# Shared output sub-tiles for the left tokens, a next-to-last q piece in two parts, and q norms by a fused multiply and sum, in an attention and feed-forward kernel

## The chip, the cores and the metric

The kernel runs on one core of one Trainium2 chip. The metric is device time in microseconds (us); lower is better. Beside the device time each execution has a *span*, from the first to the last instruction in the trace. The span is 1.7 to 2.5 us shorter than the device time in the profiled executions, and that difference is not the same for all kernels, which will matter below.

Names: PE is TensorE's matmuls and PEld its weight loads, DVE is VectorE, ACT is ScalarE, POOL is GpSimd, SP is SyncE; ACTq and SPq are DMA issues on the queues of ScalarE and SyncE.

## The reference, cut to what matters

```python
# q, k, v: (4, 5824, 256); w1, w2: (256, 1024); w3: (1024, 1024); w_out: (1024, 256)
qn = q / (norm(q, axis=1, keepdims=True) + 1e-6)     # a norm per channel, over the 5824 tokens
kn = k / (norm(k, axis=1, keepdims=True) + 1e-6)
s  = kn.transpose(0, 2, 1) @ qn / tau                # 256 x 256 per batch
a  = softmax(s, axis=-1)
x  = (v @ a).reshape(4 * 5824, 256)
out = ((x @ w1) * (x @ w2)) @ w3 @ w_out             # float32
```

The kernel folds the softmax result into w1 and w2 (so that `a` and `b` come straight from v), and w3 into w_out. Per batch there are 5824 = 45 x 128 + 64 tokens. They are worked off in 11 large chunks of 512 tokens and one small chunk of 128 + 64; the 64 are the *left* tokens.

## The kernel before

The start of batch 0: squares of q and k and their products G (the scores) on TensorE as the pieces arrive, then the *k row* (`dk` and two small fp32 matmuls, which make a row of the norms of k; it needs k's last piece), then the norm of q; all pieces of q and k are loaded first, then the weights and v. `busy(2)` is a pair of warm-up matmuls whose result nobody uses.

```python
def q_first():
    d = work.tile([P, CT, P], F32, tag="sq", name="dq", bufs=2)
    nc.vector.tensor_mul(d, S["q"], ident.unsqueeze(1).to_broadcast([P, CT, P]))
    ss = work.tile([P, CT], F32, tag="ss0", name="ss0", bufs=1)
    nc.vector.tensor_reduce(out=ss, in_=d, op=ALU.add, axis=mybir.AxisListType.X)
    st["ss"] = ss

def q_norm(src):                                   # r = 1 / (sqrt(src) + 1e-6)
    r = work.tile([P, CT], F32, tag="r", name=f"r_{n}", bufs=2)
    nc.scalar.activation(out=r, in_=src, func=AF.Ln)
    nc.scalar.activation(out=r, in_=r, func=AF.Exp, scale=0.5)
    nc.vector.tensor_scalar_add(r, r, 1e-6)
    nc.vector.reciprocal(r, r)
# ...
load_piece("q", 0, 4)
load_piece("q", 0, 5, (2, 4))
for h in range(2):
    # ... halves of w1 and w2 on the same queue, then half of v's first piece
    load_part("v", 0, 0, h * half, (h + 1) * half)
# ...
squares("k", 5, range(LAST + 1), end=True)
# ... dk, busy(2), the row of k factors
squares("q", 4, whole)
products(4, whole)
```

One step j of a chunk: two products a and b, the copy of a by ScalarE, the product by VectorE, and, two steps later, the output matmuls. PSUM tiles of a and b come from one pool of four buffers (tag "ab").

```python
def emit_ab(b, c, j):
    n = chunk_cols(c)                              # 512, or 192 in the small chunk
    # ... matmuls a and b into tiles[0], tiles[1] (tag "ab", bufs=4)
    nc.scalar.copy(a_sb[:, :n], tiles[0][:, :n])
    ab = work.tile([P, 512], BF16, tag="ab_sb", name=f"abs_{b}_{c}_{j}", bufs=8 * NDEF + 6)
    nc.vector.tensor_mul(ab[:, :n], a_sb[:, :n], tiles[1][:, :n])

def emit_out(b, c, j, ab):
    small = c == NCH - 1
    subs = [0, 64] if small else [0, 128, 256, 384]     # 0:128, and 64:192 for the 64 left ones
    for s, off in enumerate(subs):
        nc.tensor.matmul(tl[s // 2][:, s % 2, :], lhsT=ab[:, off : off + P], rhs=W_sb[:, j, :], ...)
    # at j == FT - 1, small: copy both, store rows on nc.sync (nc.scalar in the last batch),
    # then the 64 left rows on nc.sync
```

In the small chunk the second output matmul covers columns 64 to 191, of which only the last 64 are new.

## Time and profile before

| | before |
|---|---|
| device time, median of 3 | 581.64 us (581.58 to 581.91) |
| profiled execution: time, span | 581.33 us, 579.2 us |
| TensorE busy | 567.8 us, 98% |
| first softmax sum / output copy of batch 0's small chunk / last store issued | 38.12 / 190.31 / 575.95 us |

With TensorE busy nearly all the time, the questions are what the start costs before it can run, and which matmuls can go. In a line of the timeline the columns are start, duration, engine, line, operation, output and inputs, shapes and count; the bracket at the end holds the engine's idle time just before and what ended it. The lines of before stand in the prediction below; this one, from the table of 1 us stretches, shows the clock at 21 us (busy shares of PE, PEld, DVE, ACT, POOL, then granted clock, DMA share, GB/s):

```profile
21.00:22.00 1.00, 1.00 (x8) 0.82 (x7) 0.00 (x0) 0.00 (x0) 0.00 (x0) 0.50 1.04 209
```

The 0.50 is the granted clock: half speed in that microsecond. The 16 products that start at 21.21 take 3.17 us; 16 take 1.91 at full speed.

### The profile page before, as it was taken

To read this page: it belongs to the slowest core of one execution; us is meant where nothing else is said; L and a number is where in the kernel's file an instruction comes from. 1 tells how busy PE (TensorE), PEld (TensorE's weight loads), DVE (VectorE), ACT (ScalarE), POOL (GpSimd) and SP (SyncE) were. 2 spreads that over 40 slices of the span, in tenths; PEclk is the share of its full clock that TensorE was granted. 3 is DMA by queue.
4 is the path that set the end of the run, shared out by engine and by line. 5 is a ranking of instruction groups with operands and counts; after the bars stand their busy time and mean duration, and the time that the engine had idled before them with its cause. 6 is when DMAs were issued, how large, how long until landed. Compare 5 with 4: busy or idle time off the path is not lost.

```text
span 579.2 us, 10219 instructions
## 1 busy us (share of the span) xinstructions
PE 567.8 (98%) x3844; PEld 362.9 (63%) x3844; DVE 376.0 (65%) x569; ACT 341.8 (59%) x628; POOL 64.3 (11%) x141
## 2 busy tenths in 40 slices
PE   8899999999999999999999999999999999999997
PEld 4755667766666566666665666666665756665555
DVE  0047645888877667788766667778876656565564
ACT  0046535777765567677765566777665545454453
POOL 5240021110000202002000112001100000000000
PEclk9899999999999999999999999999999999999999
DMA  8999989773544899655562699754563325301011
GB/s 164 213 206 195 169 152 207 156 171 85 115 104 110 132 222 169 125 110 124 120 135 74 134 200 175 173 112 87 146 127 92 85 76 146 86 38 74 38 69 54
DMA packets 65970, 74.85 MB, mean 129 GB/s; under 512 B 45825, under 2 KB 49793, under 8 KB 65921
## 3 DMA queue, kind: packets, MB, share of 16 engines
q0 software_dynamic: 15232, 39.46, 40.0%
q1 hardware_dynamic: 50544, 34.61, 20.8%
q8 instruction: 30, 0.49, 0.3%
q14 instruction: 20, 0.16, 0.1%
q10 hardware_dynamic: 144, 0.13, 0.1%
HBM read 78.91 MB, written 23.86 MB: 177 GB/s over the span
## 4 chain that ended last, share of the span: by engine, by line
PE 90%; DMA 5%; DVE 2%; ACT 1%; issue 1%; POOL 1%; ACTq 0%; POOLq 0%
PE o L437 27%; PE a L415 26%; PE b L415 26%; PE G L188 5%; DMA q<-in_q_dram 5%; PE fold L341 2%; PE w L547 1%; ACT as L421 1%; DVE abs L423 1%; PE G L233 0%; PE sqq L221 0%; POOL k L109 0%; DVE osb L452 0%; ACT e L304 0%; PE row L269 0%
## 5 line engine op out<-in xcount | busy, mean ns | idle before, releaser
L423 DVE TENSOR_TENSOR abs<-as,b 128x512 bf16<-128x512 bf16 (+1 forms) x384 | 251.9, 658 | 153.5 <-ACT as L421 138.8
L421 ACT CAST as<-a 128x512 bf16<-128x512 f32 (+1 forms) x384 | 215.5, 562 | 173.5 <-PE a L415 85.1
L437 PE MATMUL o<-W_sb,abs 128*128 128x256 bf16 x1472 | 221.5, 273 | 0.5 <-ACT osb L451 0.4
L415 PEld LDWEIGHTS <-Wf 128*128 128x128 bf16 x1536 | 148.8, 98 | 97.2 <-issue 1.7
L415 PE MATMUL a<-vT,Wf 128*128 128x512 bf16 x704 | 209.3, 379 | 0.3
L415 PE MATMUL b<-vT,Wf 128*128 128x512 bf16 x704 | 209.4, 379 | 0.1
L437 PEld LDWEIGHTS <-abs 128*128 128x128 bf16 x1472 | 143.4, 98 | 87.0 <-issue 0.5
L197 DVE TENSOR_TENSOR acc<-acc,sq 128x1024 f32<-128x1024 f32 x66 | 80.4, 1219 | 0.1
L407 POOL COPY gate_t<-abs 1x1 bf16<-1x1 bf16 x39 | 11.2, 287 | 395.9 <-DVE abs L423 379.5
L188 PE MATMUL G<-k,q 128*128 128x256 bf16 x276 | 49.9, 273 | 0.0
L185 ACT ACTIVATE sq<-q 128x512 f32<-128x512 bf16 x66 | 41.8, 633 | 0.0
L185 ACT ACTIVATE sq<-k 128x512 f32<-128x512 bf16 x66 | 41.6, 631 | 0.0
L452 DVE COPY osb<-o 128x512 f32<-128x512 f32 x44 | 30.1, 685 | 0.4 <-PE o L437 0.4
L188 PEld LDWEIGHTS <-q 128*128 128x128 bf16 x276 | 27.0, 98 | 3.1
L451 ACT COPY osb<-o 128x512 f32<-128x512 f32 x44 | 25.7, 585 | 3.8 <-PE o L437 1.7
L271 ACT ACTIVATE kr<-row 128x256 f32<-128x256 f32 x4 | 1.5, 383 | 30.9 <-PE row L269 30.9
L341 PE MATMUL fold<-w,e 128*128 128x512 bf16 x64 | 16.5, 378 | 0.0
L109 POOL DMA_DIRECT2D q<-in_q_dram x27 | 14.5, 538 | 12.8 <-DMA q<-in_q_dram 6.4
L348 ACT ACTIVATE Wf<-fold,rs 128x512 bf16<-128x512 f32 x16 | 10.9, 687 | 7.9 <-PE fold L341 5.7
L109 POOL DMA_DIRECT2D k<-in_k_dram x25 | 13.8, 550 | 3.4 <-DMA k<-in_k_dram 1.9
L109 POOL DMA_DIRECT2D v<-in_v_dram x25 | 13.4, 537 | 6.1 <-issue 4.6
L350 DVE TENSOR_SCALAR Wf<-fold,rs 128x512 bf16<-128x512 f32 x16 | 11.8, 748 | 1.8 <-PE fold L341 1.4
(96 smaller groups left out, 177.4 us busy)
## 6 DMA issues: line engine op xcount, KB each, us to landing
out_dram<-osb SPq DMA_DIRECT2D x44, 512.0 KB, 3.0
k<-in_k_dram POOLq DMA_DIRECT2D x19, 512.0 KB, 9.5
q<-in_q_dram POOLq DMA_DIRECT2D x19, 512.0 KB, 6.2
v<-in_v_dram POOLq DMA_DIRECT2D x19, 512.0 KB, 5.4
w_wout<-in_moe_w_dram POOLq DMA_DIRECT2D x2, 1024.0 KB, 16.3
k<-in_k_dram POOLq DMA_DIRECT2D x4, 320.0 KB, 6.6
v<-in_v_dram POOLq DMA_DIRECT2D x4, 320.0 KB, 5.0
w<-in_moe_w_dram POOLq DMA_DIRECT2D x4, 256.0 KB, 7.2
```

The lines of the kernel that those rows point to most:

```text
L109: nc.gpsimd.dma_start(out=pieces[nm, n, pi][:, lo:hi, :], in_=qk_main[nm, n][0][:, pi * PIECE + lo : pi * PIECE + hi, :])
L185: nc.scalar.activation(out=dst[:, :, part, :], in_=src[:, o : o + 2, :], func=AF.Square)
L188: nc.tensor.matmul(G[:, ct, :], lhsT=qt[:, i, ct * P : (ct + 1) * P], rhs=kt[:, i, :], start=(pr == 0 and part == 0 and ct == 0), stop=(pr ...
L197: nc.vector.tensor_add(accs[n], accs[n], sqs[0])
L341: nc.tensor.matmul(st["fold", i], lhsT=st["e"][:, c2, c1 * P : (c1 + 1) * P], rhs=w12[:, c2, w, h * 512 : (h + 1) * 512], start=(c2 == 0), ...
L350: nc.vector.tensor_scalar_mul(dst, st["fold", i], st["rs"][:, c1 : c1 + 1])
L415: nc.tensor.matmul(t[:, :n], lhsT=Wf[b][:, ct, w, j * P : (j + 1) * P], rhs=rhs_of(b, c, ct), start=(ct == 0), stop=(ct == CT - 1),)
L421: nc.scalar.copy(a_sb[:, :n], tiles[0][:, :n])
L423: nc.vector.tensor_mul(ab[:, :n], a_sb[:, :n], tiles[1][:, :n])
L437: nc.tensor.matmul(tl[s // 2][:, s % 2, :], lhsT=ab[:, off : off + P], rhs=W_sb[:, j, :], start=(j == 0 and s % 2 == 0), stop=(j == FT - 1 ...
L451: nc.scalar.copy(o[:, 0:2, :], tl[0])
L452: nc.vector.tensor_copy(o[:, 2:4, :], tl[1])
```

## The change

The intent has three parts. (1) The left tokens of two batches share one sub-tile of 128 rows, so that the even batches need no second output matmul and the odd ones do a full one. (2) The next-to-last piece of q is loaded in two halves, so that its squares start sooner; three pairs of warm-up matmuls come along. (3) The q norm of batch 0 is one fused multiply-and-sum per half instead of a multiply and a reduce.

```diff
 def q_first():
-            nc.vector.tensor_mul(d, S["q"], ident.unsqueeze(1).to_broadcast([P, CT, P]))
-            nc.vector.tensor_reduce(out=ss, in_=d, op=ALU.add, axis=mybir.AxisListType.X)
+            for ct in range(CT):
+                nc.vector.tensor_tensor_reduce(
+                    out=d[:, ct, :], in0=S["q"][:, ct, :], in1=ident, scale=1.0, scalar=0.0,
+                    op0=ALU.mult, op1=ALU.add, accum_out=ss[:, ct : ct + 1],
+                )
 # emit_ab
-        nc.vector.tensor_mul(ab[:, :n], a_sb[:, :n], tiles[1][:, :n])
+        if n == 4 * P:
+            nc.vector.tensor_mul(ab, a_sb, tiles[1])
+        else:
+            nc.vector.tensor_mul(ab[:, :P], a_sb[:, :P], tiles[1][:, :P])
+            if b % 2 == 0 and j == 0:
+                lefts[b // 2] = work.tile([P, FT, 2, LEFT], BF16, tag="left", name=f"left_{b}", bufs=1)
+            nc.vector.tensor_mul(lefts[b // 2][:, j, b % 2, :], a_sb[:, P:n], tiles[1][:, P:n])
 # emit_out
-        subs = [0, 64] if small else [0, 128, 256, 384]
+        if small:
+            lhs = [ab[:, :P]]
+            if b % 2 == 1:
+                lhs.append(lefts[b // 2][:, j, :, :].rearrange("p b t -> p (b t)"))
 # ... the end of a small chunk, odd batches only
-                nc.sync.dma_start(out=out[b * N + NT * P : (b + 1) * N, :], in_=o[LEFT:, 1, :])
+                    for k in range(2):
+                        m = b - 1 + k
+                        nc.sync.dma_start(
+                            out=out[m * N + NT * P : (m + 1) * N, :], in_=o[k * LEFT : (k + 1) * LEFT, 1, :]
+                        )
 # ... the start of batch 0
     for pi in range(1, 4):
         squares("k", pi, whole)
+        busy(2)
         squares("q", pi, whole)
         products(pi, whole)
-    load_piece("q", 0, 4)
+    load_piece("q", 0, 4, (half,))
 # ...
-    squares("q", 4, whole)
-    products(4, whole)
+    for sl in (lo, hi):
+        squares("q", 4, sl)
+        products(4, sl)
```

More of the change, by code (lines that the diff above doesn't have):

```diff
@@ L46 @@
     assert moe_w_out.shape == (F, D)
-    assert T == B * N
+    assert T == B * N and B % 2 == 0
     CT = C // P
@@ L390 @@
     out_tiles = {}
+    lefts = {}
     pend = []
@@ L429, in emit_out @@
         small = c == NCH - 1
-        subs = [0, 64] if small else [0, 128, 256, 384]
+        if small:
+            lhs = [ab[:, :P]]
+            if b % 2 == 1:
+                lhs.append(lefts[b // 2][:, j, :, :].rearrange("p b t -> p (b t)"))
+        else:
+            lhs = [ab[:, i * P : (i + 1) * P] for i in range(4)]
         if j == 0:
             out_tiles[b, c] = [
-                psum.tile([P, 2, D], F32, tag="out", name=f"o_{b}_{c}_{h}", bufs=3) for h in range(len(subs) // 2)
+                psum.tile([P, 2, D], F32, tag="out", name=f"o_{b}_{c}_{h}", bufs=3) for h in range((len(lhs) + 1) // 2)
             ]
         tl = out_tiles[b, c]
-        for s, off in enumerate(subs):
+        for s, lhsT in enumerate(lhs):
             nc.tensor.matmul(
-                tl[s // 2][:, s % 2, :], lhsT=ab[:, off : off + P], rhs=W_sb[:, j, :],
-                start=(j == 0 and s % 2 == 0), stop=(j == FT - 1 and s % 2 == 1), skip_group_check=True,
+                tl[s // 2][:, s % 2, :], lhsT=lhsT, rhs=W_sb[:, j, :],
+                start=(j == 0 and s % 2 == 0), stop=(j == FT - 1 and (s % 2 == 1 or s == len(lhs) - 1)),
+                skip_group_check=True,
             )
-        clock[0] += len(subs) * (D * MM_COL + MM_FIX)
+        clock[0] += len(lhs) * (D * MM_COL + MM_FIX)
         if j == FT - 1:
@@ L446, in emit_out @@
                 nc.scalar.copy(o[:, 0, :], tl[0][:, 0, :])
-                nc.vector.tensor_copy(o[LEFT:, 1, :], tl[0][LEFT:, 1, :])
                 (nc.scalar if b == B - 1 else nc.sync).dma_start(out=rows[:, NT - 1, :], in_=o[:, 0, :])
-                nc.sync.dma_start(out=out[b * N + NT * P : (b + 1) * N, :], in_=o[LEFT:, 1, :])
+                if b % 2 == 1:
+                    nc.vector.tensor_copy(o[:, 1, :], tl[0][:, 1, :])
+                    for k in range(2):
[3 more added lines that the diff above has]
+                        )
             else:
```

## The prediction

> **What bounds the kernel now.** I read the page first (engines, slices, chain of waits), then the chain in order of time for the first 66 us, then the timeline of the start, of a batch's small last chunk and of the end, then a table of 1 us stretches for the granted clock.
>
> From the page of the kernel before:
> ```profile
> span 579.2 us, 10219 instructions
> PE 567.8 (98%) x3844; PEld 362.9 (63%) x3844; DVE 376.0 (65%) x569; ACT 341.8 (59%) x628; POOL 64.3 (11%) x141
> ...
> PE 90%; DMA 5%; DVE 2%; ACT 1%; issue 1%; POOL 1%; ACTq 0%; POOLq 0%
> ```
> TensorE is the bound: it makes up 90% of the chain that ended last. A matmul taken out after the start is worth its time, unless something takes its place. DMA has 5%: the start, where the loads of the first batch arrive.
>
> The start, from the timeline:
> ```profile
> 29.58 0.42 DVE L244 TENSOR_TENSOR dk<-sqk,ident 128x256 f32<-128x256 f32 x1 [17.80 <-PE sqk L221]
> ...
> 30.06 0.70 PE L269 MATMUL row<-dk,ones_pp 128*128 128x256 f32 x2
> ...
> 31.16 1.07 PE L221 MATMUL sqq<-q 128*128 128x128 bf16 x16 [0.40 <-DMA q<-in_q_dram]
> ...
> 35.77 0.42 DVE L249 TENSOR_TENSOR dq<-sqq,ident 128x256 f32<-128x256 f32 x1 [5.76 <-PE sqq L221]
> ...
> 36.23 0.42 DVE L251 TENSOR_REDUCE ss<-dq 128x2 f32<-128x256 f32 x1
> ...
> 36.82 0.45 PEld L132 LDWEIGHTS <-v 128*128 128x128 bf16 x8 [0.51 <-DMA v<-in_v_dram]
> ...
> 38.12 0.20 PE L320 MATMUL sum<-ones_b,e 128*128 128x1 bf16 x2 [0.67 <-ACT e L304]
> ```
> Piece 4 of q, the next to last, lands just before 31.16; from there TensorE works without a gap to the last square at 35.7. Then the q norm runs through VectorE and ScalarE until the softmax sums at 38.12. All later work hangs on these two.
>
> The small chunk of batch 0, from the timeline:
> ```profile
> 185.21 0.33 PE L415 MATMUL a<-vTt,Wf 128*128 128x192 bf16 x2
> ...
> 185.37 0.33 PE L415 MATMUL b<-vTt,Wf 128*128 128x192 bf16 x2
> ...
> 185.48 0.80 DVE L423 TENSOR_TENSOR abs<-as,b 128x192 bf16<-128x192 bf16 x2
> 185.53 0.38 PE L437 MATMUL o<-W_sb,abs 128*128 128x256 bf16 x2
> ...
> 185.75 0.33 PE L415 MATMUL a<-vTt,Wf 128*128 128x192 bf16 x2
> ```
> One step j takes 0.54 to 0.55 us of TensorE: two a, two b, and two output matmuls, of which the second yields only 64 useful rows.
>
> The end:
> ```profile
> 575.49 0.43 DVE L447 COPY osb<-o 64x256 f32<-64x256 f32 x1 [0.89 <-ACT osb L446]
> 575.95 0.49 SPq L449 DMA_DIRECT2D out_dram<-osb  x1
> ```
> The last store goes out at 575.95, and the span ends 3.2 us later.
>
> [...]
> 1. [...] the chain has eight output matmuls in 0.87 us. The 273 ns in the groups is latency, not what one costs.
> 2. [...] TensorE idles from 17.8 to 19.9, waiting for q piece 2; the granted clock is 0.68 in 20 to 21, 0.50 in 21 to 23 and 0.61 in 23 to 24, so about 3.4 us at half speed from about 20.3. The 16 products after it take 3.17 us instead of 1.91.
> 3. [...] The trace: 686 ns for 512 columns, 354 for 192 and 424 for 256[...].
> 4. [...] The build of the changed kernel shows this: four VectorE instructions, two of 128x128 and two of 128x1, stand where a multiply and a reduce stood. The trace of before has no such op.
>
> **The change part by part.**
>
> *Two batches share one sub-tile.* The second output matmul goes in batches 0 and 2: 2 x 8 = 16 fewer, 16 x 109 ns = 1.74 us less TensorE work. Batches 1 and 3 keep theirs, with full rows. In exchange each product of 192 columns becomes one of 128 and one of 64, 32 more VectorE instructions. [...] two such ops without a wait overlap by about 0.09 us in the trace (two products of 512 columns in 1.28 us, against 2 x 0.686), so the pair takes about 0.42 us against 0.354.
>
> Does TensorE feel it? A step of an even batch shrinks from 0.55 to 0.44 us. But b of step j+2 needs the PSUM buffer of b of step j, which is free once both products are done. From the timeline of batch 0: a of step 2 starts at 184.66; the copy of the large output tile keeps VectorE until 185.56; the pair for step 2 then runs from 185.48 to about 185.90. With steps of 0.44 us TensorE wants b of step 4 at 185.70 and gets it near 185.95: one stall of 0.25. I went on like this for steps 5 to 7, and each finds its buffer free by 0.05 to 0.15 us. So an even batch gains 8 x 0.109 - 0.25 = 0.62 us, and two of them 1.24. In odd batches, with 0.55 us a step, b of step 4 is at most 0.05 us late: I put them at -0.1 in sum.
>
> *q piece 4 in two parts.* At the start's 209 GB/s, half a piece (256 KB) takes 1.25 us, so the first half is there at about 29.9. TensorE then is still at the k row, which starts at 30.06 and cannot start before dk; its two fp32 matmuls free the array near 30.55. So the squares start at about 30.55 instead of 31.16. The first half is 8 x 56 + 8 x 109 ns = 1.32 us of work, until 31.87, when the second half has been there since about 31.15. Gain 0.6 us at most. POOL's issues show that each load waits for the load eight before it, so one more load puts the later issues back by one place; but the queue stays full, and I expect weights and v where they were.
>
> *Warm-up matmuls.* 3 x 2 x 0.213 = 1.28 us of work that does nothing, mostly in waits for q. [...] If the clock holds, TensorE is at k piece 5 before it lands (about 28.7), and dk comes when it came. If it still drops, the pair at piece 3, where TensorE is not waiting, puts dk back by 0.43 us, and only 0.2 of the 0.6 stays. I give the clock 60%: expected gain 0.44.
>
> *q norm fused.* Before: 35.77 to 36.65, 0.88 us. After: two of 128 columns (290 ns), overlapping little, and two accumulator reads, which I put at the 165 ns of VectorE's smallest ops here: 0.7 to 0.9 us. Gain 0.1, an estimate. It is not the halving that "fused" suggests. The earlier sums come to about 37.45, behind the v transposes, which wait for their load until 36.82 and then need 0.45 us: the start cannot gain over 0.85 us whatever the norm does.
>
> *The end.* The left rows of batches 2 and 3 leave in two stores from one queue; the issue of one took 0.49 us, so I count +0.4. Batch 2's output wait is of no account.
>
> *Sum:* -1.24 + 0.1 - 0.44 - 0.1 + 0.4 = -1.28 us. With the clock kept it is -1.44. I take 581.64 - 1.4 = 580.2 us.
>
> **The rivals.**
> (a) VectorE takes TensorE's place in the small chunks. For: 16 more ops of at least 0.13 us per pair of batches, in the stretch with the shortest steps. Against: about 0.42 us a step against 0.44. If the pair did not overlap, it would cost 0.51, and the steps of the even batches would be set by VectorE: their gain falls to 0.3 each and odd ones lose a little; total near 581.1.
> (b) The start gives nothing: the clock drops, or v comes later than 36.8, or the accumulator reads are slow. For: the DMA is at its limit to 60 us. Against: no later TensorE wait for DMA shows until the weights are in. Total near 580.9.
> (c) Everything is hidden well, the small-chunk stall does not come, and the two last stores overlap: -1.74 - 0.75 + 0.1 = -2.4, or 579.2.
> (d) The shorter even batch shifts the scheduler's clock in batch 1: the built order shows squares, products and folds of batch 1 moved by one step. TensorE is over 99% busy there, so I count 0, with 0.3 either way.
>
> **Range and chances.** The three runs of before lie within 0.33 us. My terms: small chunks -1.14 +/- 0.5, start -0.55 +/- 0.35, end +0.4 +/- 0.3, order 0 +/- 0.3: added as squares about 0.75, and a bit more for another chip. Range 579.2 to 581.3, predicted 580.2. Two per cent is 11.6 us, and no part here touches so much: 0.5% for faster, 0.5% for slower, 99% within.
>
> **What would show it.** Right: 48 output matmuls in small chunks, steps of 0.44 us in batches 0 and 2 with one stall near step 4; pairs of products in about 0.42 us; sums at about 37.5; granted clock 1.00 from 20 to 24; the last store's issue about 0.5 us behind the one before it. Wrong: steps of 0.5 us or more in even batches (rival a); the q squares not starting before 31, or the clock low at 20 to 24 (rival b); sums later than 38.1; new TensorE waits for DMA between 36 and 66 us, which would mean that the start's gain is given back to the loads; or new waits at the softmax of batches 1 to 3.

No term is cut out of the sum, which came to -1.28 us (-1.44 with the clock kept; 580.2 us was taken from that), but two terms lose a step that they were worked out with:

- The 0.42 us for a pair of products came from the formula. It stands as an estimate from lengths in the trace of before: 686 ns for 512 columns and 354 for 192 put 288 ns on 128 columns and 221 on 64, 0.51 us together, and 0.42 less the overlap of 0.09. (The changed kernel's trace has 286 and 214 ns, and 0.41 us for the pair.)
- That the warm-up pairs keep the clock up was the author's guess, at 60%, and no trace shows why they would. Of the term of 0.44 us, 0.2 does not depend on it.

The other lengths that the prediction uses are in the same trace: four output matmuls in a row take 0.44 us of TensorE (0.109 each, though the record of one is 0.27 us long), 16 squares 0.90 us from the first to what follows (31.16 to 32.06, 56 ns each), two matmuls of 512 columns 0.43 us (40.82 to 41.25, 0.215 each). The 165 ns are those of VectorE's reciprocals of 128x2 (166 ns); its memsets of one column take 59. For "the DMA is at its limit", the busy share of the DMA engines is 1.11, as the table of stretches counts it, and they move 201 GB/s, from 14.5 to 60 us. From 8.17 to 31.39 us every issue of a load on POOL that waits is released by the landing of a piece of the tensor that was issued eight loads before.

## The result, and the profile after

The changed kernel took 580.52 us (median of 4 runs, 580.28 to 580.88), the kernel before 581.77 us (4 runs, 581.58 to 582.56). Ratios in this text are the mean time of one kernel's fast runs over that of the other's of the same rounds, so not quite the ratio of the quoted medians: here 0.9976, with a 95% interval of 0.9959 to 0.9994. The result is within 2%, about a quarter per cent faster.

From the page of the changed kernel:

```profile
span 578.5 us, 10224 instructions
PE 565.4 (98%) x3826; PEld 360.8 (62%) x3834; DVE 376.8 (65%) x601; ACT 341.4 (59%) x628; POOL 64.1 (11%) x142
...
PE 89%; DMA 6%; DVE 1%; ACT 1%; issue 1%; POOL 0%; ACTq 0%; POOLq 0%
```

The span fell by only 0.7 us. PE has less to do and VectorE has 32 instructions more, and TensorE still is the chain; DMA's share rose from 5 to 6%.

The start, from the timeline of the changed kernel:

```profile
30.18 0.70 PE L272 MATMUL row<-dk,ones_pp 128*128 128x256 f32 x2 [0.30 <-DVE dk L244]
30.71 0.61 PE L221 MATMUL sqq<-q 128*128 128x128 bf16 x8
...
35.31 0.29 DVE L251 CUSTOM_DVE_ANT_0 dq<-sqq,ident 128x128 f32<-128x128 f32 x1 [5.19 <-PE sqq L221]
35.53 0.08 DVE L251 DVE_READ_ACCUMULATOR2_ANT ss<- 128x1 f32 x1
35.53 0.28 DVE L251 CUSTOM_DVE_ANT_0 dq<-sqq,ident 128x128 f32<-128x128 f32 x1
35.74 0.08 DVE L251 DVE_READ_ACCUMULATOR2_ANT ss<- 128x1 f32 x1
...
35.86 0.20 ACT L291 ACTIVATE r<-ss 128x2 f32<-128x2 f32 x1 [3.13 <-DVE ss L251]
...
37.27 0.62 PE L132 MATMUL tr_I-495_496<-ident_b,v 128*128 128x128 bf16 x8 [0.92 <-DMA v<-in_v_dram]
...
37.73 0.19 PE L323 MATMUL sum<-ones_b,e 128*128 128x1 bf16 x2
```

The squares of piece 4 follow the k row with no wait for q. The norm takes 0.55 us from the start of the first VectorE instruction to ScalarE's (35.31 to 35.86) where it took 0.91 (35.77 to 36.68). But TensorE then waits 0.92 us for v, and the sums come only 0.39 us earlier than before.

The small chunk of batch 0, from the timeline of TensorE:

```profile
184.26 0.33 PE L419 MATMUL a<-vTt,Wf 128*128 128x192 bf16 x2
184.42 0.33 PE L419 MATMUL b<-vTt,Wf 128*128 128x192 bf16 x2
184.59 0.27 PE L452 MATMUL o<-W_sb,abs 128*128 128x256 bf16 x1
184.69 0.33 PE L419 MATMUL a<-vTt,Wf 128*128 128x192 bf16 x2
...
185.13 0.33 PE L419 MATMUL a<-vTt,Wf 128*128 128x192 bf16 x2
185.43 0.32 PE L419 MATMUL b<-vTt,Wf 128*128 128x192 bf16 x2
...
185.70 0.33 PE L419 MATMUL a<-vTt,Wf 128*128 128x192 bf16 x2
...
186.18 0.33 PE L419 MATMUL a<-vTt,Wf 128*128 128x192 bf16 x2
186.48 0.32 PE L419 MATMUL b<-vTt,Wf 128*128 128x192 bf16 x2
...
186.75 0.33 PE L419 MATMUL a<-vTt,Wf 128*128 128x192 bf16 x2
```

From a to the next a is one step: 0.43, 0.44, then 0.57, 0.48, 0.57, and 0.48 to the next chunk at 187.23. The long steps have b starting 0.30 us after a instead of 0.16. The pair of products takes 0.41 us (185.14 to 185.55), as predicted.

The end:

```profile
574.16 0.42 DVE L465 COPY osb<-o 128x256 f32<-128x256 f32 x1 [0.78 <-ACT osb L462]
574.61 1.12 SPq L468 DMA_DIRECT2D out_dram<-osb  x2
```

The two stores go out one after the other. From here to the end of the span are 3.9 us, where it was 3.25 from the single store.

To see where the time went, I follow marks through the trace: points in the program at which both kernels have done the same work. The table gives how much earlier than the kernel before each run's profiled execution reached each mark (us; negative is later). Columns: the k row; the squares of q piece 4; the first VectorE instruction of the q norm; the first softmax exponential e; the transposes of v; the softmax sums; then the output copies of the small chunks of batches 0 to 3, and the span.

```
                       k row  q4 sq  norm    e    v tr   sum   b0    b1    b2    b3   span
changed kernel         -0.12  0.45   0.46  0.83  -0.44  0.39  0.93  0.71  1.40  1.34  0.70
e1_norm_only           -0.08 -0.08  -0.08  0.29  -0.05  0.29  0.29  0.29  0.29  0.29  0.30
e2_halves_only         -0.11  0.45   0.46  0.46  -0.13  0.46  0.46  0.45  0.45  0.45  0.40
e3_no_warm              0.14  0.70   0.71  0.63  -0.02  0.63  1.16  0.24  0.93  0.87  0.20
e8_shared_only         -0.17 -0.18  -0.18 -0.18  -0.16 -0.18  0.35 -0.21  0.48  0.42 -0.20
e4_v_first             -0.31  0.25   0.26  0.35   0.44  0.35  0.87  0.57  1.26  1.19  0.60
e5_two_queues          -0.15  0.41   0.42  0.48  -0.17  0.48  1.00 -0.23  0.46  0.39  0.10
e6_one_product         -0.13  0.43   0.44  0.81  -0.34  0.50  1.17  0.71  1.04  1.03  0.40
e9_long_lag            -0.34  0.23   0.24  0.29  -0.36  0.29    -     -     -    0.72  0.10
e10_all                -0.35  0.22   0.23  0.44   0.41  0.43  1.11  1.10  1.78  1.78  1.50
e11_scores_later       -0.23  0.33   0.34  0.71  -0.46  0.37  0.91  0.69  1.39  1.32  0.70
e12_norm_on_scalar     -0.36  0.21   0.22  0.43   0.39  0.42  0.96  0.89  0.37  0.31 -0.30
e13_after_again        -0.47  0.10   0.11  0.17  -0.50  0.16  0.69  0.37  1.06  0.99  0.40
```

(e9 stores its small chunks elsewhere in the order, so its marks there do not compare; b1 and b3 hold small differences of order that the next large chunks partly undo.) For the changed kernel I add up large chunk by large chunk: start +0.40, batch 0 +0.53, batch 1 -0.06, batch 2 +0.53, batch 3 -0.06, the end -0.66: 0.68 of the span of 579.2.

### The profile page after: what moved, and what is told of

The parts are those of the page before. It is cut to its first block, busy times and chain, and to the rows that moved or that the text cites. A ratio compares the mean times of both kernels' runs of the same rounds, so it can differ in the third digit from the quotient of the medians.

```text
span 578.5 us, 10224 instructions
## 1 busy us (share of the span) xinstructions
PE 565.4 (98%) x3826; PEld 360.8 (62%) x3834; DVE 376.8 (65%) x601; ACT 341.4 (59%) x628; POOL 64.1 (11%) x142
## 4 chain that ended last, share of the span: by engine, by line
PE 89%; DMA 6%; DVE 1%; ACT 1%; issue 1%; POOL 0%; ACTq 0%; POOLq 0%
PE o L452 27%; PE a L419 27%; PE b L419 26%; PE G L188 5%; DMA q<-in_q_dram 4%; PE fold L344 2%; PE w L570 1%; DMA v<-in_v_dram 1%; ACT as L425 1%; DVE abs L428 1%; POOL k L109 0%; DVE osb L473 0%; PE row L272 0%; PE ss L283 0%; ACT e L307 0%
## 5 line engine op out<-in xcount | busy, mean ns | idle before, releaser
L428 DVE TENSOR_TENSOR abs<-as,b 128x512 bf16<-128x512 bf16 x352 | 240.9, 687 | 147.5 <-ACT as L425 136.5
L452 PE MATMUL o<-W_sb,abs 128*128 128x256 bf16 x1440 | 218.2, 273 | 0.5 <-ACT osb L472 0.4
L452 PEld LDWEIGHTS <-abs 128*128 128x128 bf16 x1440 | 140.6, 98 | 86.3 <-issue 0.6
```

What stands on the lines that cost most here:

```text
L428: nc.vector.tensor_mul(ab, a_sb, tiles[1])
L452: nc.tensor.matmul(tl[s // 2][:, s % 2, :], lhsT=lhsT, rhs=W_sb[:, j, :], start=(j == 0 and s % 2 == 0), stop=(j == FT - 1 and (s % 2 == 1 ...
```

## The experiments

Twelve kernels ran, all with correct results, all with edits from the kernel before or from the changed one. One more did not build: the first form of e6 kept all its SBUF buffers and needed 79.16 kB per partition where 75.97 were left; it gave up four of them. In time, only e10 is told apart from the changed kernel. The ratios of the other repeated runs to before, 0.9974 to 0.9988, have intervals that overlap widely, so what follows about causes rests on marks and waits in single traces.

### e1: the fused norm alone (from before)

```diff
-            nc.vector.tensor_mul(d, S["q"], ident.unsqueeze(1).to_broadcast([P, CT, P]))
-            nc.vector.tensor_reduce(out=ss, in_=d, op=ALU.add, axis=mybir.AxisListType.X)
+            for ct in range(CT):
+                nc.vector.tensor_tensor_reduce(out=d[:, ct, :], in0=S["q"][:, ct, :], in1=ident, ...,
+                                               accum_out=ss[:, ct : ct + 1])
```

> The kernel before with the fused q norm alone. My theory: the four VectorE instructions give the sums 0.5 to 0.6 us after the last square (0.89 before), so the first exponential starts at about 37.2 instead of 37.56; v lands at about 36.8 as before, so its transposes are out of the way at 37.3, and the whole 0.36 us reaches the first a matmul (40.46 instead of 40.82) and every later mark. Rival: the norm was never on the path that counts (it only hides behind v): then the first a matmul stays at 40.8.

Measured: 581.02 us in one run, 581.92 for before on the same chip. The marks show the norm's effect by itself: from -0.08 at the norm to +0.29 at e, and +0.29 unchanged to the end. So the fused norm is worth 0.37 us, all of which reaches the end of the kernel when nothing else moves. One run each is too little for the time. The marks compare two traces, and the start scatters between executions, but the step from -0.08 to +0.29 lies within the norm itself.

### e2: the two halves of q piece 4 alone (from before)

```diff
-    load_piece("q", 0, 4)
+    load_piece("q", 0, 4, (half,))
-    squares("q", 4, whole)
-    products(4, whole)
+    for sl in (lo, hi):
+        squares("q", 4, sl)
+        products(4, sl)
```

> The kernel before with q piece 4 loaded and used in two halves, nothing else. My theory: the squares start at 30.7 (31.16 before) and end 0.45 to 0.55 us earlier, but the extra load puts the first v part back from 36.8 to about 37.2, so that softmax sums start near 37.7 and the first a matmul at 40.4: a gain of 0.4. Rival: the late v of the changed kernel has nothing to do with the extra load (it comes from the warm-up pairs or is jitter): then v lands at 36.8 here and the gain is 0.5 or more.

Measured: 580.87 us in one run. The row came 0.11 us later than before and the squares of q 0.45 earlier, which makes 0.56 us for the halves, and 0.45 of it is kept to the end. The number of interest is the distance between the row (which hangs on the landing of the last k piece) and the squares: 0.53 us with halves (30.18 to 30.71 in the changed kernel), 1.10 us without (before: 30.06 to 31.16).

### e3: the changed kernel without the warm-up pairs

```diff
     for pi in range(1, 4):
         squares("k", pi, whole)
-        busy(2)
         squares("q", pi, whole)
```

> The changed kernel without the three pairs of warm-up matmuls. Theory: the granted clock falls to 0.5 from about 20.3 to 23.7 as in the kernel before, but TensorE has caught up before k piece 5 lands near 28.8, so the first a matmul stays at 40.4 and the span at 578.5 within 0.2. Rival: the pairs carry part of the gain: then the k row comes 0.3 us or more later than at 30.18 and the first a matmul at 40.7 or later.

Measured: 580.74 us in one run, and the earliest row of all (+0.14). The table of 1 us stretches shows the clock; first the changed kernel, then e3:

```profile
20.00:21.00 1.00, 1.00 (x19) 0.98 (x18) 0.00 (x0) 0.00 (x0) 0.53 (x1) 1.00 1.01 201
21.00:22.00 1.00, 1.00 (x12) 0.89 (x10) 0.00 (x0) 0.00 (x0) 0.00 (x0) 1.00 1.08 217
```

```profile
20.00:21.00 1.00, 1.00 (x16) 0.94 (x14) 0.00 (x0) 0.00 (x0) 0.49 (x1) 1.00 1.03 205
21.00:22.00 1.00, 1.00 (x11) 0.90 (x10) 0.00 (x0) 0.00 (x0) 0.00 (x0) 1.00 1.05 213
```

The granted clock is 1.00 here with and without the pairs. It is 1.00 from 20 to 22 in e1, e2 and e8 too, which have no pairs either. Of these, e3 waited 2.05 us for the q piece in question, e1 1.88 and e8 2.45, about as long as the kernel before (2.10). But e2 has a drop elsewhere:

```profile
15.00:16.00 1.00, 1.00 (x12) 1.00 (x11) 0.00 (x0) 0.00 (x0) 0.36 (x1) 0.50 1.02 201
```

So of the five profiles without the pairs two have a stretch at half speed in the start, 3.41 us long in both (from 20.36 in before, from 14.31 in e2); of the nine with the pairs none has. No run shows what sets the clock, and on these counts it stays open whether the pairs keep it up. Neither drop cost anything: in both executions the row waited for the landing of k, not for the products. In the kernel before, k's last piece landed at 28.65 and its first square ran at 28.70, as close behind it as in the changed kernel (28.77 and 28.82); TensorE had caught up just in time.

### e8: the shared sub-tiles alone (from before)

The edit is the changed kernel with the norm, the halves and the warm-up pairs put back as they were.

> The kernel before with the shared sub-tile alone. Theory: no change until the small chunk of batch 0; then the marks run 0.53 us ahead after batch 0, lose 0.06 in batch 1, gain 0.53 in batch 2, are 0.95 to 1.0 ahead at the last chunk, and the two last stores give back 0.65: span 578.9 (579.2 before). Rival: the parts of the change depend on each other through the scheduler's order: then the steps of batches 0 and 2 differ from 0.53 by 0.2 or more.

Measured: 581.28 us in one run. The start is where it was (-0.18 from the k landing alone), then batch 0 gains 0.53 and batch 2 gains 0.53, as in the whole change. So the small chunks' gain does not depend on the other parts. Batch 1 lost 0.34 at a point that had no wait before. I show that point in e5, described below, where most was lost:

```profile
203.30 0.27 PE L452 MATMUL o<-W_sb,abs 128*128 128x256 bf16 x1
204.41 0.38 PE L188 MATMUL G<-k,q 128*128 128x256 bf16 x2 [0.85 <-DMA k<-in_k_dram]
```

They show TensorE at the first score product of the next batch, waiting for k. In e3 it waited 0.53 us (until 203.94), in e6 0.29 (until 203.69); in e8 the trace gives 0.18 (until 204.40), with the rest of the 0.34 just ahead of it. In the changed kernel's first profile the same product ran at 203.48 without a wait. In the four profiles with the wait the load landed between 203.7 and 204.4: in some executions part of the gain so far is handed back there.

It is tempting to say that the changed kernel comes too early for this load. The trace says otherwise: GpSimd issues the load at a point in the work, so the issue moves forward with the gain (193.65 in the changed kernel, 194.53 in the kernel before), and from issue to need there are 9.83 us in the one and 9.88 in the other. What differs is the time to the landing, as the semaphores show it: 9.22 us in before, 8.81 and 9.59 in e1 and e2, and 8.92 to 10.80 in the eleven profiles with shared sub-tiles, over 9.83 in nine of them. Whether shared sub-tiles make this load slower or chance does is not shown.

### e4: v's first part ahead of the weights (from the changed kernel)

```diff
     for h in range(2):
+        if h == 0:
+            new_piece("v", 0, 0)
+            load_part("v", 0, 0, 0, half)
         nc.gpsimd.dma_start(out=w12[:, :, 0, hs], in_=w1r[:, :, hs])
         nc.gpsimd.dma_start(out=w12[:, :, 1, hs], in_=w2r[:, :, hs])
-        if h == 0:
-            new_piece("v", 0, 0)
-        load_part("v", 0, 0, h * half, (h + 1) * half)
+        if h == 1:
+            load_part("v", 0, 0, half, PIECE)
```

> The changed kernel with the first v part issued ahead of the first two weight loads instead of behind them. Theory: v then lands near 34.8, its transposes run as soon as the warm-up matmuls after the squares are done, the sums start at about 37.3 (37.73), limited by the exponential, and the first a matmul at 40.0: 0.4 us earlier at every mark to the end, span 578.1. Rival: the weights, which now land 1.2 us later, take the place of v and hold up the first folds: gain under 0.15.

Measured: 580.32 us (580.01 to 581.07), ratio 0.9974 (0.9959 to 0.9989) to before. The transposes of v ran 0.88 us sooner than in the changed kernel, as meant, without a wait for it. But the first e came only 0.35 us ahead of before, where the changed kernel had 0.83. The sums were expected at 37.3 and came at 37.77. Of the lost 0.48, 0.20 is the later landing of k in this execution. The rest lies in the norm: r's first VectorE instruction, 0.17 us long in the kernel before, took 0.45. GpSimd was issuing the load of the output weights just then. The same showed in e3 (0.62), e5 (0.48) and e9 (0.48), and it ended 0.02 to 0.04 us ahead of the end of GpSimd's issue in each.

### e5: the last left store on a second queue (from the changed kernel)

```diff
-                        nc.sync.dma_start(
+                        (nc.scalar if b == B - 1 and k == 0 else nc.sync).dma_start(
                             out=out[m * N + NT * P : (m + 1) * N, :], in_=o[k * LEFT : (k + 1) * LEFT, 1, :]
```

> The changed kernel with the last two stores of left rows on two queues (ScalarE's and SyncE's) instead of one. Theory: the end's loss of 0.66 us comes from the second store being issued behind the first, so nearly all marks stay and the span falls by about 0.5 to 578.0. Rival: the stores themselves share the DMA engines and complete one after the other anyway: span within 0.15 of 578.5.

Measured: 580.61 us (580.20 to 581.03), ratio 0.9974 (0.9958 to 0.9991) to before. The end of e5:

```profile
575.55 0.49 SPq L468 DMA_DIRECT2D out_dram<-osb  x1
575.56 0.53 ACTq L468 DMA_DIRECT2D out_dram<-osb  x1
```

Both stores leave at once. The tail of the span lost 0.29 us to before instead of 0.60 to 0.67, so the second queue returned about 0.35. It did not show in the time; the profiled execution also held the 0.85 us wait for k shown above.

### e6: one product of 192 columns again, sub-tiles still shared (from the changed kernel)

```diff
-            nc.vector.tensor_mul(ab[:, :P], a_sb[:, :P], tiles[1][:, :P])
-            ... lefts: [P, FT, 2, LEFT]
-            nc.vector.tensor_mul(lefts[b // 2][:, j, b % 2, :], a_sb[:, P:n], tiles[1][:, P:n])
+            ... lefts: [P, FT, 2 * n]; odd batches hold their left tokens first, so the 2 x 64 adjoin
+            nc.vector.tensor_mul(ab[:, (b % 2) * n : (b % 2 + 1) * n], a_sb[:, :n], tiles[1][:, :n])
-            lhs = [ab[:, :P]] (+ the left tile in odd batches)
+            lhs = [ab[:, :P]] if b % 2 == 0 else [ab[:, P + 2 * LEFT :], ab[:, P : P + 2 * LEFT]]
```

> The changed kernel with one product of 192 columns instead of two (odd batches hold the left tokens first, so that the left halves of two batches lie side by side), with four buffers fewer for products to make room. The four PSUM buffers then rotate again so that b waits for the product of two steps before, not for ScalarE's copy of the step before. Theory 1 (the rotation alone costs the 0.34 us per even batch): batches 0 and 2 gain 0.8 or more each. Theory 2 (with steps of 0.44 us the latency of copy and product is the limit whichever buffer it is): 0.55 to 0.65 each. Odd batches should lose nothing instead of 0.06.

Measured: 580.45 us (580.11 to 581.84), ratio 0.9979 (0.9964 to 0.9993) to before. The small chunks of batch 0 gained 0.66 us and those of batch 2 0.67, and those of the odd batches lost nothing: 0.13 more per even batch and 0.06 more per odd one than with two products. (This profile waited for k of the next batch twice, 0.29 us at 203.69 and 0.18 at 337.72, so its marks fall by 0.46 and 0.35 in between.) The small chunk of batch 0 in e6, TensorE:

```profile
185.03 0.33 PE L421 MATMUL a<-vTt,Wf 128*128 128x192 bf16 x2
185.32 0.32 PE L421 MATMUL b<-vTt,Wf 128*128 128x192 bf16 x2
...
185.59 0.33 PE L421 MATMUL a<-vTt,Wf 128*128 128x192 bf16 x2
185.76 0.33 PE L421 MATMUL b<-vTt,Wf 128*128 128x192 bf16 x2
...
186.03 0.33 PE L421 MATMUL a<-vTt,Wf 128*128 128x192 bf16 x2
186.20 0.33 PE L421 MATMUL b<-vTt,Wf 128*128 128x192 bf16 x2
```

The first late b (0.29 after its a) is still there. The second one and the small ones in between are gone but for 0.08 at the last step. In the changed kernel the first late b starts at 185.43, and ScalarE's lines tell what it waited for:

```profile
184.24 0.58 ACT L472 COPY osb<-o 128x512 f32<-128x512 f32 x1
184.72 0.66 ACT L425 CAST as<-a 128x192 bf16<-128x192 f32 x2
...
186.11 0.32 ACT L425 CAST as<-a 128x192 bf16<-128x192 f32 x1 [0.25 <-PE a L419]
```

ScalarE is at the copy of the last large output tile until 184.8; the copies of a come after it and end at 185.38, 0.05 us before b starts. So the tile that this b needs was freed by a copy of a, not by VectorE. The same holds for all four late b's: they start at 185.43, 185.91, 186.48 and 186.96, each 0.05 us after such a copy ends (185.38, 185.86, 186.43, 186.91), and they wait for ScalarE's semaphore, where every b of this chunk in the kernel before waits for VectorE's. The built programs say why. Before, each b gets the buffer of an earlier b. In the changed kernel each b from step 4 on gets the buffer of the a one step earlier. In e6 only b of step 4 does; its later ones get the buffers of b's again, and their stalls go, but for the last, which follows VectorE's product. e6 takes out the extra VectorE instruction and restores the rotation at once, so the time alone does not tell the two apart; the waits do. The 0.66 us is well under the 0.8 of theory 1 and next to the range of theory 2: the order of buffers and the pair cost 0.13 of the 0.34, and 0.21 are left, of which 0.13 stand at step 4, where the buffer is still that of an a, and 0.08 at the last step.

### e9: a longer distance between product and output matmul (from the changed kernel)

```diff
+                lag = 8 if b % 2 == 0 and c >= NCH - 2 else LAG
-                while w_ready[0] and len(pend) > LAG and npop < 2:
+                while w_ready[0] and len(pend) > lag and npop < 2:
```

> The changed kernel, but in batches 0 and 2 the output matmuls of the last large chunk are held back and spread over the eight steps of the small chunk (lag of 8 instead of 2), so each small step has 0.77 us of TensorE work. Same matmuls in all. Theory: what the even batches lose is latency of copy and product behind too short steps; hidden, each gains the whole 0.87 us, 0.34 more than the changed kernel, 0.68 in sum, span 577.8. Rival: VectorE's extra instructions cost time wherever they stand, or the third large output buffer makes a new wait: gain under 0.3.

Measured: 580.87 us (580.63 to 580.93), ratio 0.9981 (0.9966 to 0.9995) to before: no better than the changed kernel. Over batch 0 the gain fell to about 0.1 and over batch 2 to 0.44. The scheduler put folds of the next batch into the small chunk, and there new waits appear, b for a copied fold among them (0.2 us). So this run does not test the latency by itself; it shows that this way of adding distance gains nothing in this schedule.

### e10: the corrections together (from the changed kernel)

One product as in e6, v first as in e4, two queues as in e5, the later scores of e11 and the norm of e12.

> The changed kernel with everything the earlier runs pointed to: one product of 192 columns in the even batches, v's first part ahead of the weights, the last left store on ScalarE's queue, the norm's r of batch 0 on ScalarE, and scores asked for two large chunks later in batches 1 to 3. My theory: first matmul of a 0.6 to 0.9 us ahead of before, +0.66 us in each of batches 0 and 2, 0 in batches 1 and 3, no wait of PE for k near 204 us, tail -0.3 us: a span of 577.3 to 577.7 us against 579.2 before, and about 0.2% under the changed kernel in time (579.3 to 579.8 us). Rival: the gains do not add, because the landing of k piece 5 sets the start and jitters by itself by half a microsecond: span 578.2 to 578.8, time 580.2 to 580.7, no different from the changed kernel.

Measured: 579.49 us (579.46 to 580.29, 5 runs), the kernel before 581.81 us (581.55 to 582.88, 9 runs), ratio 0.9958 (0.9946 to 0.9971). The changed kernel itself, as e13 in the same rounds, took 580.84 us (580.52 to 581.48). All five runs of e10 lie below all five of e13; the ratio of the means is 579.67 / 580.96 = 0.9978. The parts came as expected, but for the start: batch 0 +0.67, batch 1 -0.01, batch 2 +0.67, batch 3 0, the end -0.28, no wait for k, a span of 577.7. The later scores were needed for that: k landed 10.15 us after its issue in batch 1 and 10.52 in batch 2, more than the 9.83 that the changed kernel leaves it. The start gave 0.43 instead of 0.6 to 0.9: k landed 0.35 us later than in the profile of before, and r on ScalarE was slower than expected (see e12). The last stores of e10:

```profile
574.17 0.49 SPq L472 DMA_DIRECT2D out_dram<-osb  x1
574.17 0.54 ACTq L472 DMA_DIRECT2D out_dram<-osb  x1
```

### e13: the changed kernel once more

No edit.

> The changed kernel itself once more, so that it stands on the same chip and in the same rounds as the kernel that puts the corrections together. Every theory expects 580.2 to 580.9 us and spans of 578.5 to 579.1; it also gives a second profile of the start: if v's lateness in the first profile was chance, v lands 8.1 to 8.2 us after k piece 5 this time (it was 8.45), and then the first matmul of a comes more than 0.4 us ahead of before; if the extra q load causes it, 8.4 again.

Measured: 580.84 us (580.52 to 581.48, 5 runs), spans 578.8 to 579.7, ratio 0.998 (0.9968 to 0.9993) to before. The second profile of the same program differs at the start by as much as the experiments do: the k row came 0.35 us later than in the first profile, and v came 8.16 us after k's last piece (v's transposes at 37.33; the piece at 29.17, which I put 1.36 us ahead of the row, its distance in the first profile), where the first profile had 8.45. And here the norm met GpSimd:

```profile
36.31 0.89 POOL L537 DMA_DIRECT2D w_wout<-in_moe_w_out_dram  x1 [0.36 <-DMA w<-in_moe_w_dram]
36.45 0.20 ACT L292 ACTIVATE r<-r 128x2 f32<-128x2 f32 x1
36.68 0.48 DVE L293 TENSOR_SCALAR r<-r 128x2 f32<-128x2 f32 x1 [0.17 <-ACT r L292]
```

In the first profile of the same kernel the instruction escaped:

```profile
36.26 0.89 POOL L537 DMA_DIRECT2D w_wout<-in_moe_w_out_dram  x1 [0.36 <-DMA w<-in_moe_w_dram]
36.33 0.17 DVE L293 TENSOR_SCALAR r<-r 128x2 f32<-128x2 f32 x1 [0.17 <-ACT r L292]
```

Starting 0.07 us into the issue it took 0.17 us (in e6, 0.21 us into it, as well); starting 0.37 us into it, it took 0.48 and ended at 37.16, 0.04 us ahead of the issue's end at 37.20. My expectation of "more than 0.4 us ahead of before" at the first matmul a was missed, since both chances, k's and this one, fell on the bad side: it came 0.16 ahead.

### e11: the next batch's scores asked for later (from the changed kernel)

```diff
-            t0, t1 = 16.0, 104.0
+            t0, t1 = 18.0, 104.0
```

> The changed kernel with the scores of the next batch asked for from large chunk 18 instead of 16 in batches 1 to 3, and nothing else. My theory: the wait of PE for the k load near 204 us (0.85, 0.53, 0.29 and 0.18 us in four of the profiles) is the new limit that the changed kernel meets in some of its runs, because it reaches that point 0.9 us earlier while the load lands when it did: no such wait in this profile, all other marks as in the changed kernel, spans closer together (578.3 to 578.7). Rival: the spread of spans comes from the start (landing of the q and k pieces): spans still spread over 578.4 to 579.1.

Measured: 580.48 us (580.29 to 580.99, 4 runs), spans 578.5, 578.3, 578.5 and 578.6. No wait for k, all marks within 0.02 us of the changed kernel's from the sums on. The spans lie in 0.3 us, those of e13 in 0.9 (578.8, 579.7, 579.0, 579.1, 578.8). The 16 and 18 are the builder's own clock, in us from the start of a batch, not chunks as the expectation has it; the first score product moved from 203.48 to 206.10. In this profile k landed at 203.98, half a microsecond after the changed kernel needed it, so the edit did spare a wait here. That the k wait makes the spread of the spans is not shown: the five spans of e10, with the same later scores, lie in 0.9 us (577.6 to 578.5), and those of the kernel before, which has no such wait in its profile, in 1.3 (579.5 to 580.8). In the time (ratio 0.9975 to before, 0.998 for e13) the two kernels are not told apart.

### e12: v first, and r wholly on ScalarE (from the changed kernel)

```diff
+            if n == 0:
+                nc.scalar.activation(out=r, in_=r, func=AF.Ln, bias=eps_t)
+                nc.scalar.activation(out=r, in_=r, func=AF.Exp, scale=-1.0)
+            else:
-            nc.vector.tensor_scalar_add(r, r, 1e-6)
-            nc.vector.reciprocal(r, r)
+                nc.vector.tensor_scalar_add(r, r, 1e-6)
+                nc.vector.reciprocal(r, r)
```

> The changed kernel with v's first part loaded ahead of the weights, and r of batch 0 computed wholly on ScalarE (logarithm, then exponential), so that VectorE has no instruction in the window in which GpSimd issues the output weights' load. My theory: VectorE's small r instruction of 0.45 to 0.62 us, where it took 0.17 in the kernel before, was held up by GpSimd's issue; without it the first e comes 1.45 to 1.5 us after the last squares start, whatever GpSimd does (1.42 without and 1.70 to 1.87 with the holdup on VectorE), and the rest of batch 0 follows about 0.25 us sooner than with v's part alone. Rival: the wait moves to ScalarE's second instruction or to the k factors, and the first e comes 1.7 us or more after.

Measured: 581.46 us (580.57 to 582.17, 4 runs), ratio 0.9988 (0.9974 to 1.0002) to before: the worst of all. The norm itself did what it should in kind and half of it in size:

```profile
35.55 0.29 DVE L251 CUSTOM_DVE_ANT_0 dq<-sqq,ident 128x128 f32<-128x128 f32 x1 [5.19 <-PE sqq L221]
...
36.20 0.89 POOL L543 DMA_DIRECT2D w_wout<-in_moe_w_out_dram  x1 [0.32 <-DMA w<-in_moe_w_dram]
...
36.57 0.29 ACT L294 ACTIVATE r<-r,eps_t 128x2 f32<-128x2 f32 x1
36.90 0.20 ACT L295 ACTIVATE r<-r 128x2 f32<-128x2 f32 x1
37.13 0.91 ACT L311 ACTIVATE e<-s,r 128x256 bf16<-128x256 f32 x2
```

1.58 us from the norm's start to e, against 1.42 in the changed kernel's first profile (35.31 to 36.73), 1.73 in e13 (35.66 to 37.39) and 1.70 in e4. ScalarE was not held as VectorE had been: its exponential, inside GpSimd's issue (36.20 to 37.09) but for its last 0.01 us, took its usual 0.20 us. But the logarithm with a bias took 0.29 us, not the 0.20 I had reckoned with; the k factors show the same 0.09 us in every batch of the kernel before (0.51 with the bias, 0.42 without). So it removes the chance and saves 0.12 us against e4, not 0.25. The kernel then lost 1.05 us in batch 2: it waited 0.89 us for the first k piece of batch 3,

```profile
338.25 0.38 PE L188 MATMUL G<-k,q 128*128 128x256 bf16 x2 [0.89 <-DMA k<-in_k_dram]
```

the same wait one batch later, with 10.84 us from the load's issue to its landing. e10, which has the same norm and the later scores of e11, has no such wait in either batch.

## Why the prediction was right or wrong, point by point

The predicted 580.2 us (579.2 to 581.3) held: 580.52 measured, and 580.84 in the second set. Within it, two terms were off in opposite directions.

**Shared sub-tiles: size near, mechanism partly wrong.** Predicted +0.62 per even batch and -0.05 per odd one; measured +0.53 and -0.06, alone (e8) and in the whole. The 8 x 0.109 us per batch came off, as the saving of 0.66 plus the remaining stalls in e6 shows: 0.87 less 0.13 at the first late b less 0.08 at the last. The prediction's step "one stall of 0.25, then each finds its buffer free" failed. It took b of step j+2 to need the buffer of b of step j; from step 4 on it needs that of the a one step earlier. There are two stalls of 0.13 and two of 0.04, 0.34 in sum, and each ends with ScalarE's copy of a, not with VectorE's pair, whose 0.41 us was predicted well. So 0.53 near 0.62 is partly luck. The steps average 0.525 us over the last four, for which rival (a) had VectorE as the limit; VectorE is not the limit there. About 0.13 us per even batch is the price of the pair and of the order of buffers that came with it.

**q in two parts: right.** Predicted 0.6 at most; 0.57 us measured from the k row. The trace of the changed kernel shows 0.45 only because its k piece landed 0.12 us later than the one in the profile of before.

**Warm-up matmuls: the step was idle.** The prediction gave the clock 60%, and counted 0.44 of the 0.6 for it. The clock did hold, but it held in e1, e3 and e8 without the pairs too, and the drops in the profiles of before and e2 did not delay the row. A good or a harm of the pairs is not shown. The reason for the discount was read from a single execution.

**Fused norm: mis-sized.** Predicted 0.1; it measured 0.36 (0.91 to 0.55). The accumulator reads take 0.08 us, not the 0.165 put in for them, and they overlap with the next fused instruction, which starts at the same time (both at 35.53). e1 shows that the whole 0.37 can reach the end.

**The cap by v: right, and it bound.** The prediction said that the start cannot gain more than 0.85 because v's transposes wait for their load. e came 0.83 earlier and the sums 0.39: v was later than the prediction's "where they were". That step failed in the profiled execution, by 0.44 us, 0.12 of which is the later k piece: TensorE waited 0.92 us for v where it had waited 0.51, so the start's gain was in part given back to a load, the sign that the prediction had named for 36 to 66 us. In eight profiles with the extra load and the weights ahead of v (both of the changed kernel, e2, e3, e5, e6, e9 and e11) v came 8.15 to 8.45 us after k's last piece; in three without it (before, e1, e8) 8.11 to 8.13. So the extra load may cost v 0.02 to 0.3 us; most of the scatter is between executions of one program, and how much belongs to which stays open.

**The end: right, in the span and in device time.** Predicted -0.4, give or take 0.3. In the span the end lost 0.66. But the span is not the metric. Device time less the time at which the first store of left rows is issued is 5.38 us in the kernel before (581.33 - 575.95; its only one) and 5.67 in the changed one (580.28 - 574.61), 0.29 more. Of the profiles without shared sub-tiles all three have 5.36 to 5.38; of those with them and one queue seven have 5.65 to 5.75 (e12 has 5.93 and e4 6.32); with two queues they are 5.29 and 5.48. What device time holds outside the span, the traces do not show. In device time the terms are 0.40 + 0.53 - 0.06 + 0.53 - 0.06 - 0.29 = 1.05 us, the difference of the two profiled executions (581.33 - 580.28). This sum closes by construction, since the end is what the issue of the store leaves over.

**Order in batch 1: right for the order, and a new wait that the prediction looked for in the wrong place.** Nothing was lost to the order. Besides the longer wait for v, one came that it had not named, at 204 us (and 338 us), for k of the next batch. It takes up to 0.9 us back in some executions. It is not there because TensorE comes earlier, since the issue comes earlier too (see e8); it is there when the load takes more than 9.83 us, and e11 and e10 escaped it by needing k later.

**A chance the prediction did not have:** the faster start moved r's VectorE instruction into GpSimd's issue of the output weights' load. There, in five profiles (e3, e4, e5, e9 and e13), a 0.17 us instruction took 0.45 to 0.62 and ended within 0.04 us of the issue's end; not so in that of the kernel before, where r ran after the issue. What holds it the traces do not show, and it is not the whole of the issue's recorded span (0.89 us, and rough on GpSimd): additions that began 0.07, 0.17 (e11) and 0.21 us into the issue were not held, those at 0.23 (e3) and 0.37 to 0.40 were, and one at 0.74 (e2) was not. Nor was the reciprocal behind an addition that escaped: it began 0.27 to 0.41 us into the issue in the changed kernel, e11 and e6, and took 0.17 us. So not every VectorE instruction is held. No run moved GpSimd's issue alone.

## What to carry to other kernels

When several small gains are stacked, a load that used to arrive in time can become the next limit, as v did at the start (TensorE waited 0.92 us for it, 0.51 before); look for the first wait of the bound engine on DMA in every stage, not only in the stage that was changed. But before putting such a wait down to the change, compare the time from the load's issue to its need with the time to its landing: at 204 us the first had not changed (9.83 us against 9.88). Before splitting one instruction in two, check which pool buffers are now freed in which order: here the pair and the order that came with it cost 0.13 us per even batch together, and all four late b's waited for a copy of a, none for the pair. And read a feature of the profile, such as a clock drop or a landing time, from several executions before building on it; here the k row, which follows the landing of one load, lay between 0.14 us before and 0.47 us after that of the kernel before, with the same loads ahead of it, as much as any part of the change was worth.
